# A second DMA queue for the weight tiles converted beside attention, in a float64-weight attention and gated-MLP kernel

## The chip, the cores and the metric

One Trainium2 chip, one core of it. The metric is the device time of one launch in microseconds. Five engines run programs of their own in order: TensorE (PE, with its weight loads as PEld), VectorE (DVE), ScalarE (ACT), GpSimd (POOL) and SyncE (SP). A data transfer is an instruction of the engine that begins it; the 16 DMA engines then move the bytes.

## The reference

Batch 4, 12 heads, 448 positions, head size 64, so 1792 tokens of width 768:

```python
scores = q @ k.T / sqrt(64) - log(448)
x = (sigmoid(scores) @ v) laid out as (1792, 768)
h = x @ w_in;  x = (h * cos(h)) @ w_out                   # w_in 768 x 2048
g = x @ w_gate; x = (silu(g) * (x @ w_val)) @ w_out2       # 768 x 1536, 1536 x 768
```

q, k and v are float32. The weights are float64, eight bytes an element, and the kernel must turn them into float32 itself.

## The kernel before

**Stages.** Attention comes first, in 24 steps of two heads each ("pairs", the loop in `attention`). Then layer 1 (two halves of the tokens, eight chunks of w_in and w_out each) and layer 2 (two halves, six chunks). TensorE does every float32 product as three products of a high and a low part; the layers use a seven-product scheme for 2 x 2 blocks (`seven`), and its sums of weight blocks are made by `combine` (L509) on VectorE or GpSimd.

**Conversion of weights.** `conversions` (L419) takes one tile of 128 x 768 float64 at a time from a list in order of need: it loads the raw words (768 KB, `move`, L235), scales the low words on ScalarE, takes the absolute value of the high words on VectorE or ScalarE (`absolute`, L409), does four more steps on VectorE, and stores 384 KB of float32 to a scratch tensor in HBM. There are 68 such tiles. Later `loads` brings float32 tiles back from scratch and `operands` splits them.

Some of it runs beside attention: `lend_pool` (L388) lends four pairs of buffers (`lr` raw, `lt` result) and starts four copies of `conversions` that get them as `raw`, `t` and `back`. Each copy converts tile after tile in its own buffers until it sees `stop`, which is set after pair 17; after pair 21 the buffers' memory is used for something else. Copies without `back` start after attention, with two raw buffers.

**What sets the order of instructions.** A planner (`Order`) runs while the program is written. Every task yields an engine with a planned cost, or a wait; `run` takes the task that could start first by the plan (then the lowest rank) and emits its instruction. What one engine does is therefore a fixed list. Attention's own instructions are written out by hand, and `beside` (L633, called at L778 and L781) tells the planner how long they hold each engine in a pair of planned length 5.8: SyncE for the first 2.0, VectorE for 1.75, ScalarE until 4.55 and again for 0.55 at the end. The planner fills what is left. Planned time starts at 0, the first pair at 6.0. A transfer of `move` is planned as 0.8 of SyncE, and what it brings as there 5.0 later.

**Attention's transfers.** `load` (L702) brings the queries and keys of a pair (`rqk`, two halves, four buffers) and its values (`vs`, five buffers) three pairs ahead, and `load_last` the last value rows of six pairs, all begun by SyncE except one half at the very start that ScalarE begins. `split` (L720) makes high and low parts on VectorE (L723, L724), `scores` (L734) and `weigh` (L748) are TensorE's work of a pair, and the sigmoid (L738) is ScalarE's.

Of the kernel before, what the change touches and what calls it, by code (L numbers as in the profile page):

```python
# [11 lines left out]
I32 = mybir.dt.int32  # L12
# [138 lines left out]
def block_kernel(  # L151
# [11 lines left out]
    nc = tc.nc  # L163
    P = 128
    B, NP, D, _, _, S = qk.shape
# [15 lines left out]
    def f32(ap):  # L181
        return ap.bitcast(F32)

    def flat(ap):
        return ap.rearrange("p k c -> p (k c)")
# [40 lines left out]
    def act(time, **kw):  # L226
        return {"ACT": time}, lambda _: nc.scalar.activation(**kw)  # L227

    def vec(time, out, in0, in1, op):
        return {"DVE": time}, lambda _: nc.vector.tensor_tensor(out=out, in0=in0, in1=in1, op=op)  # L230
# [4 lines left out]
    def move(out, in_):  # L235
        return {"SP": 0.8}, lambda _: nc.sync.dma_start(out=out, in_=in_)

    LANDING = 5.0
    PAIR = 5.8
    ENDS = ((17, 21),)  # L240
# [89 lines left out]
    def by(time, step):  # L330
        return (*step, time)
# [56 lines left out]
    def lend_pool():  # L388

        pool = tc.tile_pool(name="ln", bufs=1, side="right")  # L390
        ln, stop, backs = pool.__enter__(), [], []
        for a in range(4):
            raw = ln.tile([P, WT, 2], I32, tag=f"lr{a}", name=f"lr{a}")
            t = ln.tile([P, WT], F32, tag=f"lt{a}", name=f"lt{a}")
            backs.append(order.event())
            order.spawn(conversions(raw, t, backs[-1], stop), end)

        def swap():
            assert all(back.time is not None for back in backs)
            pool.__exit__(None, None, None)  # L400
            xr = ctx.enter_context(tc.tile_pool(name="xr", bufs=1, side="right"))
            x1 = xr.tile([P, 3 * size + 2 * WT + 32], F32R, tag="x1", name="x1")
            give_x(x1, ORDER[4:])
            pairs.give(x1[:, 3 * size + 16:3 * size + 16 + 2 * WT].rearrange("p (m a k c) -> p m a k c", m=2, a=2, k=KH))
            x_open.set()

        return stop, swap

    def absolute(t, words):  # L409
        def do(engine):  # L410
            if engine == "ACT":
                nc.scalar.activation(out=t, in_=words.bitcast(F32), func=AF.Abs)
            else:
                nc.vector.tensor_scalar(
                    t.bitcast(I32), words, 0, 0x7FFFFFFF, op0=ALU.logical_shift_left, op1=ALU.bitwise_and
                )
        return {"ACT": 0.9, "DVE": 0.58}, do

    def conversions(raw=None, t=None, back=None, stop=None):  # L419

        while not stop:
            w, f = next(todo, (None, 0))
            if w is None:
                break
            if not back:
                raw = yield raws
            time = uses[id(w), f]
            yield move(raw.rearrange("p n two -> p (n two)"), flat(w[f]).bitcast(I32))
            yield LANDING
            yield by(time, act(0.9, out=raw[:, :, 0], in_=raw[:, :, 0].bitcast(U32), func=AF.Copy, scale=2.0 ** -29))  # L430
            if not back:
                t = yield convs
            ti = t.bitcast(I32)
            yield by(time, absolute(t, raw[:, :, 1]))
            yield by(time, ({"DVE": 0.56}, lambda _: nc.vector.tensor_scalar(
                t, t, HI_MOST, HI_LEAST, op0=ALU.min, op1=ALU.max
            )))
            yield {"DVE": 0.56}, lambda _: nc.vector.tensor_scalar(
                ti, ti, 3, 0x3FFFFFF8, op0=ALU.logical_shift_left, op1=ALU.bitwise_and
            ), time  # L440
            yield {"DVE": 0.96}, lambda _: nc.vector.scalar_tensor_tensor(
                out=ti, in0=raw[:, :, 1], scalar=-0x40000000, in1=ti,
                op0=ALU.bitwise_and, op1=ALU.bitwise_or,
            ), time
            yield by(time, vec(0.97, ti, ti, raw[:, :, 0], ADD))
            if not back:
                raws.give(raw)
            there = scratch[id(w), f]
            there[0] = dram.tile([P, KD * P], F32, tag=f"s{names[id(w)]}{f}", name=f"s{names[id(w)]}{f}")
            yield move(there[0], t)  # L450
            order.spawn(landed(there[1], None if back else t), 0)
        if back:
            yield LANDING
            back.set()
            return

        raw = yield raws
        room = raw.rearrange("p n two -> p (n two)").bitcast(F32)
        free_t.give((yield convs))
        if not ended:  # L460
            ended.append(True)
            free_t.give(room[:, :WT])
            free_t.give(room[:, WT:])
        else:
            for a in range(3):
                tmps.give(room[:, a * N:(a + 1) * N])

    def landed(event, t=None):
        if t is not None:
            yield 3.0  # L470
            convs.give(t)
            yield LANDING - 3.0
        else:
            yield LANDING
        event.set()
# [30 lines left out]
    def operands():  # L506
# [16 lines left out]
        def lower(keys, s, t, lo, hi, size, room, free, done):  # L523
# [10 lines left out]
            if kept:  # L534
                there = dram.tile(list(s.shape), F32, tag=f"k{len(stash)}", name=f"k{len(stash)}")
                stash[at] = there, order.event()
                yield {"SP": 0.8}, (lambda _: nc.sync.dma_start(out=there, in_=f32(s))), due[keys[0]]
                yield LANDING
                stash[at][1].set()
# [17 lines left out]
        def here(keys, s, room, done):  # L557
            yield LANDING
            for i, key in enumerate(keys):
                event = made_event(key)  # L560
                made[key][1] = (s, i, room)
                event.set()
# [485 lines left out]
    with tc.manual_schedule():  # L1048
        nc.gpsimd.memset(warm, 0.0)
        for s in range(n_stages):  # L1050
            order.spawn(inputs(s), 3.5)
        order.spawn(loads(), 3)
        order.spawn(operands(), 4)
        order.spawn(banker(), 2)
        attention()
        with tc.tile_pool(name="mp", bufs=1) as mp:
            for i in range(2):
                raws.give(mp.tile([P, WT, 2], I32, tag=f"raw{i}", name=f"raw{i}"))
                order.spawn(conversions(), end)
            convs.give(mp.tile([P, WT], F32, tag="cv", name="cv"))  # L1060
            convs.give(ring[:, 2])
            make_pairs(mp, 3, "b")
            mp.tile([P, 16], F32, tag="pad", name="pad")
            for i in range(4):
                gslots.give(mp.tile([P, 2, N], F32R, tag=f"g{i}", name=f"g{i}"))
            for i in range(6):
                (tmps if i < 5 else rounds).give(mp.tile([P, N], F32, tag=f"u{i}", name=f"u{i}"))
            free_t.give(mp.tile([P, WT], F32, tag="t3", name="t3"))
            order.spawn(tensor_engine(), 0)
            order.run()  # L1070
            assert not order.open
# [51 lines left out]
```

## Time and profile before

| | us |
|---|---|
| median of 3 runs | 1088.21 |
| lowest, highest | 1086.23, 1089.68 |
| the profiled execution | 1090.07 |
| its span, first to last instruction | 1087.9 |

| engine | busy us | share |
|---|---|---|
| PE | 1067.5 | 98% |
| DVE | 846.4 | 78% |
| ACT | 664.3 | 61% |
| POOL | 126.4 | 12% |

The profile page gives busy time by engine over the span; a stretch of the span can be asked for by itself, and there the granted TensorE clock (1.00 is full speed) and the share of the DMA engines' time stand beside it. The chain of waits follows the work that ended last back to its start. A timeline lists one engine's instructions in order, with the idle time before each in square brackets and what ended it. An engine name with q (SPq) is the engine's queue of instructions that begin transfers.

### The profile page before, as it was taken

Reading aid. Unit: us, or ns where it says so; the run is one execution under the profiler, and the core shown is the slowest. Engines: PE = TensorE matmul, PEld = TensorE weight load, DVE = VectorE, ACT = ScalarE, POOL = GpSimd, SP = SyncE. Lnnn points to the kernel's source line nnn. Section 1 sums busy time; section 2 is a strip of 40 time slices with the busy share of each in tenths; the row PEclk is TensorE's granted clock in tenths of the full one; section 3 lists DMA queues with packets and bytes.
Section 4 is the critical chain, followed back from the end, with each engine's and each line's share of the span. In section 5 each row is a group of like instructions: output and inputs, shape, how many; then the busy total and the mean of one; then the engine's idle time right before and its main releaser. Section 6 shows DMA issues by size and latency. Waiting matters only on the chain.

```text
span 1087.9 us, 14759 instructions
## 1 busy us (share of the span) xinstructions
PE 1067.5 (98%) x5507; PEld 930.7 (86%) x5507; DVE 846.4 (78%) x1138; ACT 664.3 (61%) x1005; POOL 126.4 (12%) x97
## 2 busy tenths in 40 slices
PE   8999999999999899999997999999999999999998
PEld 4554569999989799999997999999999999999997
DVE  4969759989999989989899988887559644655644
ACT  6787768877777777777776665554345444433330
POOL 0100003001111101100023111111111110110100
PEclk9999999999999999999998999999999999999999
DMA  9999524545654146454513566565122322112002
GB/s 260 300 268 238 155 87 146 201 148 174 218 203 146 58 170 206 161 175 145 189 59 132 176 213 205 189 194 171 43 73 76 124 78 73 59 45 73 30 1 102
DMA packets 64455, 156.68 MB, mean 144 GB/s; under 512 B 10112, under 2 KB 36736, under 8 KB 64384
## 3 DMA queue, kind: packets, MB, share of 16 engines
q1 hardware_dynamic: 64240, 155.51, 45.3%
q8 instruction: 43, 0.70, 0.3%
q10 hardware_dynamic: 144, 0.23, 0.1%
q14 instruction: 28, 0.23, 0.1%
HBM read 123.47 MB, written 32.24 MB: 143 GB/s over the span
## 4 chain that ended last, share of the span: by engine, by line
PE 86%; DVE 9%; DMA 2%; issue 1%; ACT 1%; SPq 1%; DVEq 0%; ACTq 0%
PE banks L1000 42%; PE banks L902 33%; PE banks L748 6%; PE banks L734 5%; DVE x L230 2%; DVE r L230 2%; DMA rqk<-in_qk 2%; DVE u L230 1%; DVE g L230 1%; DVE wa L230 1%; DVE wb L230 0%; DVE u L816 0%; DVE s L230 0%; DVE x L660 0%; SPq L707 0%
## 5 line engine op out<-in xcount | busy, mean ns | idle before, releaser
L902 PE MATMUL banks<-g,wb 128*128 128x448 f32 x1044 | 224.5, 363 | 1.1 <-ACT g L227 0.5
L1000 PE MATMUL banks<-x,wb 128*128 128x448 f32 x1044 | 225.0, 363 | 0.1
L902 PEld LDWEIGHTS banks<-g,wb 128*128 128x128 f32 x1044 | 195.6, 188 | 15.8 <-ACT g L227 1.4
L1000 PEld LDWEIGHTS banks<-x,wb 128*128 128x128 f32 x1044 | 195.9, 188 | 14.6 <-ACT banks L227 0.5
L902 PE MATMUL banks<-g,wa 128*128 128x448 f32 x720 | 159.9, 369 | 9.9 <-ACT g L227 8.4
L1000 PE MATMUL banks<-x,wa 128*128 128x448 f32 x738 | 160.6, 363 | 0.0
L902 PEld LDWEIGHTS banks<-g,wa 128*128 128x128 f32 x720 | 137.6, 192 | 21.4 <-ACT g L227 9.1
L1000 PEld LDWEIGHTS banks<-x,wa 128*128 128x128 f32 x738 | 138.3, 188 | 11.1 <-issue 0.7
L227 ACT ACTIVATE u<-u 128x448 f32<-128x448 f32 x179 | 99.4, 570 | 38.9 <-DVE u L230 26.3
L230 DVE TENSOR_TENSOR u<-u,banks 128x448 f32<-128x448 f32 x119 | 73.4, 617 | 58.2 <-PE banks L1000 54.8
L230 DVE TENSOR_TENSOR r<-banks,r 128x896 f32<-128x896 f32 (+1 forms) x69 | 74.2, 1076 | 53.4 <-PE banks L902 52.9
L738 ACT ACTIVATE a<-banks 128x896 f32<-128x896 f32 x96 | 82.7, 922 | 20.6 <-PE banks L734 12.1
L230 DVE TENSOR_TENSOR wb<-t,wb 128x768 fp32r<-128x768 f32 x73 | 69.5, 957 | 14.8 <-ACT wb L227 14.4
L227 ACT ACTIVATE g<-u 128x448 fp32r<-128x448 f32 x97 | 55.1, 572 | 39.8 <-DVE u L230 24.7
L1000 PE MATMUL banks<-x,s 128*128 128x448 f32 x360 | 79.3, 364 | 0.0
L734 PEld LDWEIGHTS banks<-qk 64*128 64x128 f32 x576 | 50.3, 185 | 31.2 <-ACT a L738 9.4
L512 POOL TENSOR_TENSOR sum<-t 128x384 f32<-128x384 f32 x20 | 36.6, 1832 | 339.7 <-DMA t<-swi 147.3
L227 ACT ACTIVATE wb<-t 128x768 fp32r<-128x768 f32 x73 | 60.8, 836 | 24.5 <-PE banks L1000 17.7
L734 PE MATMUL banks<-qk 64*128 64x448 f32 x576 | 69.4, 382 | 4.7 <-ACT a L738 2.6
L227 ACT ACTIVATE r<-banks 128x896 f32<-128x896 f32 x52 | 47.8, 919 | 40.6 <-PE banks L902 40.6
L1000 PEld LDWEIGHTS banks<-x,s 128*128 128x128 f32 x360 | 67.5, 187 | 5.3
L227 ACT ACTIVATE banks<-banks 128x448 f32<-128x448 f32 x80 | 42.3, 529 | 47.6 <-PE banks L1000 46.6
(103 smaller groups left out, 1474.5 us busy)
## 6 DMA issues: line engine op xcount, KB each, us to landing
raw<-in_w_out SPq DMA_DIRECT2D x23, 768.0 KB, 5.0
t<-swi SPq DMA_DIRECT2D x32, 384.0 KB, 3.2
t<-swo SPq DMA_DIRECT2D x64, 192.0 KB, 2.7
rqk<-in_qk SPq DMA_DIRECT2D x47, 224.0 KB, 8.1
raw<-in_w_gate SPq DMA_DIRECT2D x12, 768.0 KB, 4.7
raw<-in_w_val SPq DMA_DIRECT2D x12, 768.0 KB, 4.6
t<-swg SPq DMA_DIRECT2D x18, 384.0 KB, 3.0
t<-swd SPq DMA_DIRECT2D x34, 192.0 KB, 2.8
```

Source lines behind the costliest of these rows:

```text
L227: return {"ACT": time}, lambda _: nc.scalar.activation(**kw)
L230: return {"DVE": time}, lambda _: nc.vector.tensor_tensor(out=out, in0=in0, in1=in1, op=op)
L512: on.tensor_tensor(out=out, in0=a, in1=b, op=op)
L734: nc.tensor.matmul(sc[:, j], lhsT=both[half, m, 1, starts[c]:starts[c] + P], rhs=both[half, p, 0], start=n == 0, stop=n == 2,)
L738: nc.scalar.activation(out=a, in_=sc, func=AF.Sigmoid, bias=-math.log(S), scale=1.0 / math.sqrt(D))
L748: nc.tensor.matmul(o[half], lhsT=value, rhs=a[:, j], start=c == 0, stop=c == NCH)
L902: nc.tensor.matmul(banks[:, first + e - d, :N], lhsT=w[:, m, e % KH, :], rhs=g[:, p], start=(i, m, p) == (0, 0, 0) and is_fresh and not pr ...
L1000: nc.tensor.matmul(bank, lhsT=w[:, m, k, :], rhs=x[:, k, p, :], start=(k, m, p) == (0, 0, 0) and i in (1, 5), stop=(k, m) == (KH - 1, 1), ...
```

## The change

The raw load and the store of a tile converted beside attention (a copy of `conversions` that has `back`) are begun by GpSimd, with a planned cost of 1.1 of GpSimd; those of the tiles converted after attention stay with SyncE.

```diff
+    def move_beside(out, in_):
+        return {"POOL": 1.1}, lambda _: nc.gpsimd.dma_start(out=out, in_=in_)
+
...
             time = uses[id(w), f]
-            yield move(raw.rearrange("p n two -> p (n two)"), flat(w[f]).bitcast(I32))
+            convey = move_beside if back else move
+            yield convey(raw.rearrange("p n two -> p (n two)"), flat(w[f]).bitcast(I32))
             yield LANDING
...
-            yield move(there[0], t)
+            yield convey(there[0], t)
             order.spawn(landed(there[1], None if back else t), 0)
```

## Rows read from the trace of the kernel before

**Rows 1.** The page, part 4: shares of the chain that ended last.

```profile
PE 86%; DVE 9%; DMA 2%; issue 1%; ACT 1%; SPq 1%; DVEq 0%; ACTq 0%
```

**Rows 2.** Busy time by stretch; the stretch's length first, then engines, clock, DMA share.

```profile
0.00:155.00 155.00, 149.15 (x972) 77.97 (x973) 114.42 (x136) 113.00 (x142) 5.51 (x9) 0.99 0.82 217
...
320.00:400.00 80.00, 75.80 (x367) 69.66 (x366) 75.14 (x96) 60.88 (x96) 11.89 (x9) 0.98 0.36 117
...
585.00:620.00 35.00, 29.33 (x135) 26.38 (x134) 30.68 (x42) 23.46 (x37) 13.95 (x6) 0.90 0.55 192
```

**Rows 3.** Timeline of PE in attention: start, length, line, count, idle time before.

```profile
28.77 0.47 PE L734 MATMUL banks<-qk 64*128 64x448 f32 x2
29.78 2.63 PE L734 MATMUL banks<-qk 64*128 64x448 f32 x22 [0.54 <-DVE qk L724]
...
94.60 2.83 PE L734 MATMUL banks<-qk 64*128 64x448 f32 x24
97.36 2.48 PE L748 MATMUL banks<-a,vs 128*64 128x448 f32 x12
...
104.76 1.28 PE L734 MATMUL banks<-qk 64*128 64x448 f32 x6 [2.15 <-ACT a L738]
105.97 3.68 PE L748 MATMUL banks<-a,vs 128*64 128x448 f32 x12
```

**Rows 4.** Who waited for whom, 0 to 150 us: total, times, longest.

```profile
DVE qk L723 <- DMA rqk<-in_qk: 19.4, 8, 5.4
...
ACT x L658 <- DVE r L230: 2.8, 1, 2.8
```

**Rows 5.** Timeline of DVE in attention.

```profile
8.37 0.63 DVE L723 CAST qk<-rqk 128x896 fp32r<-128x896 f32 x1 [0.92 <-DMA rqk<-in_qk]
...
75.20 0.63 DVE L723 CAST qk<-rqk 128x896 fp32r<-128x896 f32 x1 [3.69 <-DMA rqk<-in_qk]
...
85.31 1.55 DVE L660 CAST x<-r 128x1344 fp32r<-128x1344 f32 x1
```

**Rows 6.** Timeline of SP's queue in attention.

```profile
7.36 1.48 SPq L707 DMA_DIRECT2D rqk<-in_qk  x2
...
9.95 2.67 SPq L236 DMA_DIRECT2D lr<-in_w_in  x4
...
18.60 3.98 SPq L707 DMA_DIRECT2D rqk<-in_qk  x2
...
26.86 0.34 SPq L236 DMA_DIRECT2D swi<-lt  x1
```

**Rows 7.** Instructions on the lent raw buffers: count, ns, first and last start.

```profile
L227 ACT ACTIVATE lr<-lr x13: 922/934/953, 16.7 to 115.0; 128x768 int32<-128x768 uint32 x13
```

**Rows 8.** VectorE's instructions on the lent result buffers: least, median, most ns.

```profile
L435 DVE TENSOR_SCALAR lt<-lt x13: 551/554/1361, 18.8 to 122.8; 128x768 f32<-128x768 f32 x13
...
L441 DVE SCALAR_TENSOR_TENSOR lt<-lr,lt x13: 950/957/959, 20.0 to 124.0; 128x768 int32<-128x768 int32 x13
```

**Rows 9.** Early stretches as in rows 2; DMA share and GB/s are last.

```profile
2.80:3.40 0.60, 0.60 (x4) 0.18 (x2) 0.00 (x0) 0.12 (x1) 0.00 (x0) 1.00 1.05 370
3.40:4.40 1.00, 1.00 (x4) 0.41 (x3) 0.00 (x0) 0.00 (x0) 0.00 (x0) 1.00 1.07 231
14.00:16.00 2.00, 2.00 (x14) 0.72 (x10) 0.00 (x0) 0.92 (x1) 0.00 (x0) 1.00 1.03 410
```

**Rows 10.** DMA queues from 2.8 to 3.4 us: packets, MB, share (q10 ScalarE's, q1 SyncE's).

```profile
q10 hardware_dynamic: 100, 0.15, 68.1%
q1 hardware_dynamic: 38, 0.07, 37.1%
```

**Rows 11.** Timeline of POOL.

```profile
49.17 1.44 POOL L512 TENSOR_TENSOR sum<-t 128x384 f32<-128x384 f32 x1 [48.33 <-DMA t<-swi]
50.69 1.74 POOL L512 TENSOR_TENSOR t<-t 128x384 f32<-128x384 f32 x1
```

**Rows 12.** Timeline of DVE beside it.

```profile
49.78 1.78 DVE L724 TENSOR_TENSOR qk<-rqk,qk 128x896 fp32r<-128x896 f32 x1
```

## The prediction, made before the changed kernel had run

> **What bounds the kernel now.** I read the page's chain first. 86% of it is TensorE [rows 1], so a change counts only where TensorE stands still. The busy times by stretch show where that is: the 155 us of attention hold 149.15 us of PE, the stretch around 360 us lacks 4.2 us and the one around 600 us 5.67 us [rows 2]; the rest of the span up to the last stage has next to nothing. The change touches transfers of attention only, so I took the timeline of PE there. After the first pairs it has two marks [rows 3]. At 28.77 a score group that takes 2.83 us elsewhere lasts until 32.41, 0.81 us lost, because a split waited for its queries and keys. At 104.76 PE had been idle for 2.15 us, and the twelve products behind it take 3.68 us where 2.48 is usual, 1.20 us more: TensorE had stood still, and for a moment it ran slower. Together 4.16 us.
>
> Both marks lead to SyncE's queue. VectorE's splits waited 19.4 us in eight places for `rqk` [rows 4], among them 3.69 us at 75.20 [rows 5]. From there to the stop at 104 VectorE has no gap longer than an instruction's start, its work on the layers' input begins only at 85.31 [rows 5], and ScalarE's part of that waits 2.8 us for it [rows 4], with a sigmoid behind it that TensorE needs. The splits waited since SyncE begins everything in one order: four raw tiles stand ahead of later pairs' loads, a pair of load instructions takes 3.98 us to get rid of at 18.60, and the first store holds the queue until 26.86 [rows 6]. The DMA engines are full at this time (a share of 1.03 to 1.07 [rows 9]).
>
> **The change, part by part.**
>
> *Removed from SyncE:* 13 raw loads and 13 stores [rows 7], with their waits. Then attention's loads wait for free buffers alone, and are begun up to three pairs ahead. I expect the waits of 19.4 us to go mostly. At 28.77 that repays 0.81. At 104 it repays the 3.69 us that VectorE lost at 75.20, and 1.9 us of that reach the input work: pairs last (94.60 - 29.58) / 11 = 5.91 us [rows 3], so pair 13 began at 82.8, and the result that the work needs was there some 0.6 later, not at 85.31. Of 2.15 us some 0.25 stays idle, and the slow stretch of 1.20 goes. Sum -3.9; bounds 0 (the waits move from queries to raw tiles, as the DMA engines are no less full) and -4.16. What is late next there is ScalarE, which the plan gives one conversion instruction a pair.
>
> *Moved, the first four raw tiles.* They depend on nothing. On SyncE they come behind four pairs' loads, at 9.95 [rows 6]; as the first work of GpSimd after a small memset they begin at about 1 us, and 4 x 0.79 MB lie beside the very loads that the first pairs wait for. One queue alone moves attention's rows at 231 GB/s and the big rows of raw tiles at 410; the only moment with two queues moved 370 [rows 9]. So a second queue adds throughput, but it also takes turns. If SyncE's queue keeps 231 GB/s, the cost is 0. If the raw tiles go first, it is 3.15 MB / 410 GB/s = 7.7 us. In between: if a row of each goes in turn, a row of 1792 bytes lasts 77 ns at 370/16 GB/s an engine and one of 6144 bytes 240 ns at 410/16, so SyncE gets 1792/317 ns x 16 = 90 GB/s. Pair 1's loads behind the first (192 + 448 KB, 0.66 MB) then last 7.3 us instead of 2.8; its split, which started at 8.37 [rows 5], comes 4.5 us later, with no slack, as its scores follow pair 0's at once. The raw tiles are through by about 13 us, so pair 2 pays no more. In the one row of two queues they were not served alike, 100 packets to 38 [rows 10], so neither end is excluded. I take 4.0, near the middle, because GpSimd's first transfer also needs its own start. A stop of that length is followed by a slow stretch like that at 104.76: +1.2, bounds 0 and 2.4 (two stops).
>
> *The trains of conversion.* Planned starts follow from the code: SyncE was reserved to 2.0 of each pair, so the four loads were planned inside pair 0 and ScalarE's first step fell in pair 1 (16.7 [rows 7]). GpSimd is unreserved, the loads are planned at 0.15, 1.25, 2.35 and 3.45, and the first step fits pair 0. Everything then runs a pair earlier, until VectorE turns to the input work. By the stop after pair 17 nine stores had been planned, so 4 + 9 tiles were taken; a tenth now fits before the input work, and I expect 14. The extra one is 3.6 us of VectorE (two steps of 0.957 us and three of 0.554 [rows 8]) in attention, where VectorE has 155 - 114.4 = 40.6 us idle [rows 2]: nothing. Later, 54 tiles in place of 55 are converted over some 586 us; the two places where TensorE lacks time (80 and 35 us [rows 2]) are 20% of that, 0.2 x 3.6 = 0.7. I take -0.7; but another tile count makes the planner order all the rest anew, so the bounds are -4.2 (the first place cleared) and +5.7 (a second one like 600).
>
> *Added to GpSimd:* 28 transfers. No row shows one begun there. The nearest are its own combines, 1.44 and 1.74 us [rows 11], and SyncE's store, 0.34 us [rows 6]; at 0.3 to 1.7 us each they fill 9 to 49 us of a GpSimd that is busy 5.51 us of 155 [rows 2]. I take 1.1 each, the plan's own figure. A store on GpSimd waits for the last VectorE step of its tile; behind it stand the same buffers' next load, harmless with four pairs of buffers, and a combine for the first weight blocks, which nothing in attention needs. A combine waiting as at 49.17 (its tile landed late [rows 11]) holds raw loads back by a microsecond or two. Cost 0; without the cover of four buffers ScalarE and TensorE would wait that long, about 2 us.
>
> Sum: -3.9 + 4.0 + 1.2 - 0.7 + 0 = +0.6 against the profiled 1090.07, so 1090.7. That execution lies 1.86 above the median of 1088.21, hence 1088.8.
>
> *A rule against it.* Beside GpSimd's second combine VectorE's split step took 1.78 us [rows 12], and one conversion step 1361 ns where 554 is the median [rows 8]: the two engines hold each other up by 0.7 to 0.8 us. The Trainium skill, SBUF — State Buffer, Who interferes with whom, goes further: a transfer begun by GpSimd is itself starved while VectorE runs certain one-input instructions in its two-port mode, and the advice is to begin it on another engine. No row here shows that for a transfer. As a mechanism of this kernel it is the third rival.
>
> **The rivals.**
>
> 1. *Free start, faster.* SyncE's queue keeps its 231 GB/s beside GpSimd's, or GpSimd begins late. For it: two queues moved 370 GB/s [rows 9]. Against it: 100 to 38 [rows 10]. Then no 4.0 and no 1.2: -4.2 - 0.7 = -4.9, 1083.3.
> 2. *Raw tiles first, slower.* Place: pairs 0 to 2. Price 7.7, and two slow stretches, 2.4; since TensorE is then later than everything else, the 4.16 goes entirely: 7.7 + 2.4 - 4.2 - 0.7 = +5.2, 1093.4. It decides from a start cost of some 7 us, where it passes what the later stops give back by 0.3%. Against it: the first loads are under way before GpSimd's.
> 3. *Ports, slower.* Each transfer costs VectorE 0.7 us. From 75.2 to 104 is five pairs with 28/20 transfers each, 7 x 0.7 = 4.9 us where VectorE has no gap, so the stop at 104 is not repaid but grows: +0.6 + 3.9, about 1092.7.
> 4. *Nothing changes hands.* The waits for queries turn into waits for raw tiles, TensorE's stops stay, the start is free: 1088.2. It counts with "same".
> 5. *Another order.* The later stages come out anew by up to -4 or +5 around any of these.
>
> **Chances.** Forecast and 4: 0.37. Rival 1, and forecast with a lucky order: 0.35. Rivals 2, 3 and an unlucky order: 0.13, 0.08, 0.07. A difference of 0.3%, 3.3 us, is about what can be told from no change: faster 0.35, same 0.37, slower 0.28. The likeliest case alone runs from 1085.5 to 1091.5; with both sides 1080 to 1097.
>
> **What would show it.** A second queue of 28 transfers, 16 MB, from about 1 us; SyncE's queue without stores; splits' waits for `rqk` after 28 us near 0; PE idle around 10 us and none at 28 and 104; 14 tiles in `lr`, the first ScalarE step near 10 us. Wrong would be: pair 1's split before 9 us (start free), VectorE's conversion steps above their medians throughout (ports), 13 tiles, or a changed loss around 360 and 600 us larger than attention's.

## The result: 1.1% slower, and the profile after

| | us |
|---|---|
| before, median of 6 runs | 1087.55 |
| changed kernel, median of 6 runs (1098.21 to 1100.47) | 1099.89 |
| ratio, with its 95% interval | 1.011 (1.0096 to 1.0124) |
| the profiled execution of the changed kernel, and its span | 1099.17, 1097.4 |

The prediction was 1088.8 in a range of 1080 to 1097: wrong, by 11 us.

The changed kernel's page, part 3, shows that the change does what it says: a queue of its own (q0) carries 16.52 MB, 28 transfers of 14 tiles.

```profile
q1 hardware_dynamic: 60208, 139.00, 39.7%
q0 software_dynamic: 3136, 16.52, 4.3%
```

Its busy time by stretch has the columns of [rows 2]. The place near 360 us lacks 4.65 us where it lacked 4.2, the place near 600 us lacks 12.16 where it lacked 5.67, and attention's clock has fallen to 0.97.

```profile
0.00:155.00 155.00, 146.59 (x957) 79.54 (x959) 117.85 (x142) 114.02 (x141) 21.45 (x36) 0.97 0.77 224
...
320.00:400.00 80.00, 75.35 (x359) 69.14 (x358) 73.81 (x96) 61.51 (x96) 16.95 (x9) 0.96 0.31 99
...
585.00:620.00 35.00, 22.84 (x104) 20.41 (x103) 29.99 (x41) 21.63 (x33) 6.48 (x4) 0.80 0.44 150
```

The timeline of PE, to be read against [rows 3]: the stops at 28 and 104 us are gone, and one of 4.98 us at the start and one of 11.57 us near 600 stand in their place. The first line after the second "..." is pair 2's scores, the next the first products of layer 1, so attention's end; L1004 is what was L1000, L738 what was L734.

```profile
7.46 4.05 PE L738 MATMUL banks<-qk 64*128 64x448 f32 x22 [0.65 <-DVE qk L728]
16.48 0.74 PE L738 MATMUL banks<-qk 64*128 64x448 f32 x2 [4.98 <-DVE qk L727]
17.52 4.30 PE L738 MATMUL banks<-qk 64*128 64x448 f32 x22 [0.29 <-DVE qk L728]
...
24.91 2.84 PE L738 MATMUL banks<-qk 64*128 64x448 f32 x24
...
157.95 2.09 PE L1004 MATMUL banks<-x,wa 128*128 128x448 f32 x9
...
587.34 1.98 PE L1004 MATMUL banks<-x,s 128*128 128x448 f32 x9
600.89 0.74 PE L906 MATMUL banks<-g,wa 128*128 128x448 f32 x1 [11.57 <-ACT g L227]
602.22 3.84 PE L906 MATMUL banks<-g,wa 128*128 128x448 f32 x11 [0.59 <-DVE g L230]
```

The same marks in the kernel before:

```profile
16.40 2.09 PE L734 MATMUL banks<-qk 64*128 64x448 f32 x18
...
154.71 2.09 PE L1000 MATMUL banks<-x,wa 128*128 128x448 f32 x9
...
584.27 1.98 PE L1000 MATMUL banks<-x,s 128*128 128x448 f32 x9
591.89 5.04 PE L902 MATMUL banks<-g,wa 128*128 128x448 f32 x12 [5.64 <-ACT g L227]
```

Mark against mark the changed kernel is 8.5 us late at pair 2, 3.24 at the end of attention, 3.07 ahead of the stop near 600 us, 9.0 behind it, and 9.5 at the end of the span. So two places carry it: the start of attention, of which a part is given back, and the stop near 600 us, which no transfer of the change comes near. The medians lie 12.3 apart, these two executions 9.1: the one of before was 2.5 us above its median in the table, the one of the changed kernel 0.7 below. From 25 to 155 us TensorE is now busy for all of the 130 us (127.31 before), and VectorE's splits wait 1.8 us for `rqk` from 25 to 150 us (13.7 before).

What the start is can be read from three views of the changed kernel. GpSimd begins four raw tiles at 1.31 us and is done with it by 3.6 (where [rows 6] had SyncE begin them at 9.95):

```profile
1.31 2.27 POOL L239 DMA_DIRECT2D lr<-in_w_in  x4 [0.45 <-issue]
24.21 0.83 POOL L239 DMA_DIRECT2D swi<-lt  x1 [20.63 <-DVE lt L230]
```

Pair 1's split starts at 15.71 where [rows 5] had it at 8.37:

```profile
15.71 0.63 DVE L727 CAST qk<-rqk 128x896 fp32r<-128x896 f32 x1 [8.31 <-DMA rqk<-in_qk]
```

And the DMA queues from 8 to 10 us (packets, MB, share, as in [rows 10]) move almost the same number of packets each, but 0.54 MB against 0.16:

```profile
q0 software_dynamic: 104, 0.54, 76.8%
q1 hardware_dynamic: 107, 0.16, 26.8%
```

### The profile page after: what moved, and what is told of

The parts are those of the page before. It is cut to its first block, busy times and chain, and to the rows that moved or that the text cites. A ratio compares the mean times of both kernels' runs of the same rounds, so it can differ in the third digit from the quotient of the medians.

```text
span 1097.4 us, 14796 instructions
## 1 busy us (share of the span) xinstructions
PE 1068.0 (97%) x5507; PEld 934.1 (85%) x5507; DVE 850.5 (78%) x1132; ACT 663.4 (60%) x1002; POOL 156.2 (14%) x134
## 3 DMA queue, kind: packets, MB, share of 16 engines
q0 software_dynamic: 3136, 16.52, 4.3%
## 4 chain that ended last, share of the span: by engine, by line
PE 92%; DVE 5%; DMA 1%; issue 1%; ACT 0%; SPq 0%; DVEq 0%
PE banks L1004 44%; PE banks L906 36%; PE banks L752 7%; PE banks L738 6%; DVE x L230 1%; DMA rqk<-in_qk 1%; DVE r L230 1%; DVE u L230 1%; DVE g L230 0%; DVE u L820 0%; ACT x L662 0%; DVE wb L230 0%; DVE s L230 0%; DVE wa L230 0%; SPq L711 0%
## 5 line engine op out<-in xcount | busy, mean ns | idle before, releaser
L1004 PE MATMUL banks<-x,wb 128*128 128x448 f32 x1044 | 225.0, 363 | 0.1
L1004 PEld LDWEIGHTS banks<-x,wb 128*128 128x128 f32 x1044 | 195.7, 188 | 14.6 <-ACT banks L227 0.5
L1004 PE MATMUL banks<-x,wa 128*128 128x448 f32 x738 | 160.6, 363 | 0.0
L1004 PEld LDWEIGHTS banks<-x,wa 128*128 128x128 f32 x738 | 138.3, 188 | 11.1 <-issue 0.7
L738 PEld LDWEIGHTS banks<-qk 64*128 64x128 f32 x576 | 53.4, 194 | 32.8 <-ACT lr L227 8.5
L1004 PE MATMUL banks<-x,s 128*128 128x448 f32 x360 | 79.3, 364 | 0.0
L738 PE MATMUL banks<-qk 64*128 64x448 f32 x576 | 71.7, 394 | 7.2 <-DVE qk L727 6.3
L1004 PEld LDWEIGHTS banks<-x,s 128*128 128x128 f32 x360 | 67.5, 187 | 5.3
L230 DVE TENSOR_TENSOR g<-u,g 128x448 fp32r<-128x448 f32 x98 | 63.7, 658 | 8.5 <-ACT g L227 8.4
```

Source lines behind the costliest of these rows:

```text
L738: nc.tensor.matmul(sc[:, j], lhsT=both[half, m, 1, starts[c]:starts[c] + P], rhs=both[half, p, 0], start=n == 0, stop=n == 2,)
L1004: nc.tensor.matmul(bank, lhsT=w[:, m, k, :], rhs=x[:, k, p, :], start=(k, m, p) == (0, 0, 0) and i in (1, 5), stop=(k, m) == (KH - 1, 1), ...
```

## The experiments

Each was timed in five rounds beside the kernel before, the last one excepted. "Order" is the order of instructions that the planner writes.

**The order without the queue, and the queue without the order.** Three kernels. `e1_order` keeps the changed kernel's plan and gives the transfers back to SyncE:

```diff
     def move_beside(out, in_):
-        return {"POOL": 1.1}, lambda _: nc.gpsimd.dma_start(out=out, in_=in_)
+        return {"POOL": 1.1}, lambda _: nc.sync.dma_start(out=out, in_=in_)
```

> The changed kernel's order on TensorE, VectorE and ScalarE, and its 14 tiles, but the lent tiles' transfers are begun by SyncE again (planned as before-change GpSimd work at 1.1). Theory O (two costs: the early raw loads hold up pair 2's queries, about 3 us; and the tile count of 14 gives the later stages another order, whose stop near 600 us grows from 5.6 to 11.6 us): the stop near 600 us is 9 to 12 us here too, and from the end of attention to the end of the span it is 6 us longer than before. At the start ScalarE's first conversion step now stands ahead of pair 1's sigmoids while its tile lands at some 16 us, so attention itself may lose 2 to 5 us for another reason; the time 1094 to 1100. Rival Q (the later loss comes from GpSimd's queue or from ports, not from the order): the stop near 600 us is 5 to 6 us as before, the time 1087 to 1092.

`e2_queue` keeps the plan of before and gives the transfers to GpSimd:

```diff
     def move_beside(out, in_):
-        return {"POOL": 1.1}, lambda _: nc.gpsimd.dma_start(out=out, in_=in_)
+        return {"SP": 0.8}, lambda _: nc.gpsimd.dma_start(out=out, in_=in_)
```

> The order and the 13 tiles of the kernel before (planned as SyncE's work at 0.8), but the lent tiles' transfers are begun by GpSimd. Theory O: a stop of 4 to 6 us for pair 2's queries at about 12 us as in the changed kernel, the stops of before at 28 and 104 us gone, attention 2 to 4 us longer than before, everything later as before: 1089 to 1092. Rival Q: later stages lose 6 us although their order is that of before: 1096 to 1100. Rival P (ports): VectorE's conversion steps in attention above their medians of 554 and 957 ns.

`e3_thirteen` is the changed kernel with a limit:

```diff
         while not stop:
+            if back:
+                taken.append(True)
+                if len(taken) > 13:
+                    break
             w, f = next(todo, (None, 0))
```

> The changed kernel with one edit: no more than 13 tiles are taken beside attention. Theory O: the later stages have the order of before again, so the stop near 600 us is 5 to 6 us, the start pays as in the changed kernel: 1088 to 1092, 8 to 11 us under the changed kernel. Rival Q: 1097 to 1100 as the changed kernel.

| | median us | ratio to before, 95% |
|---|---|---|
| e1_order | 1099.1 | 1.0090 (1.0066 to 1.0113) |
| e2_queue | 1094.3 | 1.0049 (1.0033 to 1.0066) |
| e3_thirteen | 1094.37 | 1.0049 (1.0033 to 1.0066) |

The stop near 600 us follows the tile count and not the queue. It is 11.56 us in `e1_order`, whose lent transfers are SyncE's:

```profile
599.84 0.74 PE L906 MATMUL banks<-g,wa 128*128 128x448 f32 x1 [11.56 <-ACT g L227]
```

and 5.64, that of before, in `e3_thirteen`, whose transfers are GpSimd's:

```profile
596.72 5.25 PE L912 MATMUL banks<-g,wa 128*128 128x448 f32 x12 [5.64 <-ACT g L227]
```

One tile fewer takes 1099.89 - 1094.37 = 5.5 us off the changed kernel; by the two ratios, each to the kernel before of its own rounds, it is 6.6. `e2_queue` and `e3_thirteen` agree with each other: that is the price of the queue alone, 6.0 us by the medians and 5.3 by the ratios, above what both expectations gave (1089 to 1092 and 1088 to 1092). `e1_order` is as slow as the changed kernel through a coincidence that its expectation allowed for: with ScalarE's first step planned in pair 0 and its tile landing late, a sigmoid queued behind it holds TensorE for 5.75 us until 18.21 us (ScalarE itself waits 4.91 us for that tile). The rival that the later loss needs GpSimd's queue is refuted. So is the ports' rival; it is taken up below.

**14 tiles without any of it.** `e6_before14` is the kernel before with one number changed.

```diff
-    ENDS = ((17, 21),)
+    ENDS = ((18, 21),)
```

> The kernel before with one number changed, so that the lent buffers stop taking tiles a pair later (18 in place of 17): 14 tiles, every transfer begun by SyncE, the start untouched. The order of the layers on TensorE is then that of the changed kernel. Theory O: the stop near 600 us is 11 to 12 us, attention's length as before, 1092 to 1096. Rival Q (that stop needs GpSimd's queue or the late start): 5 to 6 us there, 1086 to 1090.

Measured: 1094.03, ratio 1.0064 (1.0043 to 1.0085). The timeline of PE:

```profile
338.82 0.47 PE L902 MATMUL banks<-g,wa 128*128 128x448 f32 x1 [2.82 <-ACT g L227]
...
594.87 0.74 PE L902 MATMUL banks<-g,wa 128*128 128x448 f32 x1 [11.56 <-ACT g L227]
```

The stops at 340 and near 595 us are those of the changed kernel to a hundredth or two (2.83 and 11.57). A fourteenth tile by itself costs 6 us; no transfer changed hands.

What fills the longer stop can be read on VectorE, which has no gap in it in either kernel. In the changed kernel (the stop is from 589.32 to 600.89) three splits of weight blocks and four steps of conversions lie inside it, 5.45 us together:

```profile
589.25 0.95 DVE L230 CUSTOM_DVE_ANT_0 t<-raw,t 128x1536 uint16<-128x1536 uint16 x1
590.12 0.55 DVE L439 TENSOR_SCALAR cv<-cv 128x768 f32<-128x768 f32 x1
...
592.59 0.95 DVE L230 TENSOR_TENSOR x<-t,x 128x768 fp32r<-128x768 f32 x1
593.46 0.95 DVE L230 TENSOR_TENSOR wb<-t,wb 128x768 fp32r<-128x768 f32 x1
...
594.86 0.95 DVE L230 TENSOR_TENSOR wa<-t,wa 128x768 fp32r<-128x768 f32 x1
...
597.33 0.55 DVE L442 TENSOR_SCALAR cv<-cv 128x768 int32<-128x768 int32 x1
...
598.34 0.55 DVE L417 TENSOR_SCALAR t<-raw 128x768 int32<-128x768 int32 x1
```

In the kernel before (the stop is from 586.25 to 591.89) three such splits come ahead of it, and one conversion step lies at its end:

```profile
583.31 0.94 DVE L230 TENSOR_TENSOR x<-t,x 128x768 fp32r<-128x768 f32 x1
584.17 0.95 DVE L230 TENSOR_TENSOR wb<-t,wb 128x768 fp32r<-128x768 f32 x1
...
585.58 0.94 DVE L230 TENSOR_TENSOR wa<-t,wa 128x768 fp32r<-128x768 f32 x1
...
591.13 0.94 DVE L230 CUSTOM_DVE_ANT_0 t<-raw,t 128x1536 uint16<-128x1536 uint16 x1
```

The stop grew by 5.93 us. `e6_before14` has the changed kernel's seven instructions inside its stop too.

**Is a tile more what hurts, or any other order?** `e9_twelve` is the kernel before with the limit above set to 12, `e10_before15` the kernel before with another rank for conversions:

```diff
-                uses.setdefault((id(w), 2 * c + i), due[key] - 25.0)
+                uses.setdefault((id(w), 2 * c + i), due[key] - 15.0)
```

> The kernel before, but no more than 12 tiles are taken beside attention; all transfers by SyncE. If a tile more beside attention is what hurts the layers, 12 are better than 13: 1083 to 1087. If it is only that the planner makes another order, for which the kernel's numbers were not chosen, 12 may be as bad as 14: the stops of TensorE after attention sum to more than the 10 us of before, 1091 to 1098.

> The kernel before with one number of the plan changed: the rank of a tile's conversion is its use less 15 in place of less 25. No transfer changes hands. If the layers' loss is a matter of the order that the planner falls into, this gives other stops after attention too; in its order TensorE should wait in three places (near 307, 360 and 587 us) in place of five. 1084 to 1089, faster if the place near 587 us stays at 5 to 6 us.

`e9_twelve` took 1099.8, ratio 1.0089 (1.0062 to 1.0116), above its range at the top. TensorE stops in six places after attention; the longest:

```profile
232.93 0.47 PE L908 MATMUL banks<-g,wa 128*128 128x448 f32 x1 [2.10 <-ACT g L227]
...
375.54 0.74 PE L908 MATMUL banks<-g,wa 128*128 128x448 f32 x1 [5.42 <-ACT g L227]
...
602.38 5.25 PE L908 MATMUL banks<-g,wa 128*128 128x448 f32 x12 [5.64 <-ACT g L227]
```

`e10_before15` took 1087.21, ratio 0.9987 (0.9972 to 1.0003): no difference that counts. Its two stops:

```profile
362.76 0.74 PE L902 MATMUL banks<-g,wa 128*128 128x448 f32 x1 [4.46 <-ACT g L227]
...
589.06 5.13 PE L902 MATMUL banks<-g,wa 128*128 128x448 f32 x12 [5.64 <-ACT g L227]
```

So neither more nor fewer tiles is good in itself: by the medians 12 cost 11.8 us and 14 cost 6.0 against 13 (9.7 and 7.0 by the ratios). The planner writes another order for each, and of the three orders tried beside this kernel's two were slower and one no different.

**What the queue costs at the start.** `e8_small` is `e2_queue` with the first four raw loads cut into quarters of their columns.

```diff
+    def move_parts(out, in_):
+        def do(_):
+            n = in_.shape[1] // 4
+            for part in range(4):
+                cols = slice(part * n, (part + 1) * n)
+                nc.gpsimd.dma_start(out=out[:, cols], in_=in_[:, cols])
+        return {"SP": 0.8}, do
...
-            yield convey(raw.rearrange("p n two -> p (n two)"), flat(w[f]).bitcast(I32))
+            if back:
+                taken.append(True)
+            yield (move_parts if back and len(taken) < 5 else convey)(raw.rearrange("p n two -> p (n two)"), flat(w[f]).bitcast(I32))
```

> As the run with the order of before and GpSimd's queue, but each of the first four raw loads is begun as four transfers of a quarter of the columns, rows of 1536 bytes in place of 6144. If the two queues take turns row by row, SyncE's rows now get half the bytes: pair 1's split starts at 9 to 12 us (15.7 there), pair 2's scores at 17 to 20 us (25.7 there), the time 1086 to 1090. If GpSimd's queue is served first whatever the rows: 14 us or later, 1092 to 1096.

Measured: 1092.0, ratio 1.0039 (1.0024 to 1.0053), 2.3 us under `e2_queue` by the medians and 1.1 by the ratios, whose intervals overlap, so the gain in time is not shown. In the profiles pair 1's split moves from 15.71 to 12.07, pair 2's scores from 25.67 to 22.55, attention's end from 158.71 to 155.63: the direction of turns row by row, but less than expected. The queues of `e8_small` from 8 to 10 us:

```profile
q0 software_dynamic: 97, 0.32, 65.0%
q1 hardware_dynamic: 115, 0.19, 38.2%
```

GpSimd's packets now hold 0.32 MB / 97 = 3.3 KB in place of the changed kernel's 0.54 / 104 = 5.2 KB, not 1.5: the rows were a quarter as long but the packets did not shrink as much. The packet counts stay near one to one, and SyncE's queue goes only from 80 to 95 GB/s. That the two queues alternate packet by packet fits both runs from 6 us on; why the packets hold two rows is open. Nor does this run change the rows alone: GpSimd begins the 16 parts one after another until 14.68 us, from the ninth on after waiting for earlier ones to land, where `e2_queue` had begun all four tiles by 3.56. And from 4 to 6 us SyncE's queue moved 0.22 MB where it had moved 0.04 in `e2_queue`, so part of the gain lies ahead of the even turns.

**What of SyncE's queue made the queries late?** `e7_stores` gives GpSimd only the 13 stores, in the order of before. `e4_queue_start` gives it the stores and all raw loads but the first four.

```diff
# e7_stores
-            yield move(there[0], t)
+            yield (move_beside if back else move)(there[0], t)
# e4_queue_start
-            yield convey(raw.rearrange("p n two -> p (n two)"), flat(w[f]).bitcast(I32))
+            if back:
+                taken.append(True)
+            yield (move_first if back and len(taken) < 5 else convey)(raw.rearrange("p n two -> p (n two)"), flat(w[f]).bitcast(I32))
```

Here `move_beside` costs SyncE 0.8 in the plan and is begun by GpSimd; `move_first` is `move`.

> The kernel before with its order, in which GpSimd begins the 13 stores alone; the raw loads stay with SyncE. If SyncE's waits for stores are what made the queries late, the stops at 28 and 104 us shrink and attention is 1 to 4 us shorter: 1084 to 1087.5. If the raw tiles ahead of them in the ring are: no change, 1087 to 1089.5.

> As the run with the order of before, but the first four raw loads stay with SyncE, behind four pairs' loads; the other 9 raw loads and all 13 stores are begun by GpSimd. Theory O: no stop at 12 us, and the stops at 28 and 104 us are smaller or gone: attention 1 to 4 us shorter than before, 1083 to 1087. If the later stops were not SyncE's doing: 1087 to 1089. Rival P: 1090 and more.

`e7_stores`: 1088.69, ratio 1.0003 (0.9991 to 1.0015). Its stop of attention is still there:

```profile
105.17 0.87 PE L737 MATMUL banks<-qk 64*128 64x448 f32 x6 [1.93 <-ACT a L741]
```

`e4_queue_start`: 1089.76, ratio 1.0006 (0.9992 to 1.0019), short of the expected 1083 to 1087. The stop at 104 us is gone, and others have come at 54 and 61 us. Ahead of the first VectorE waits 4.60 us for queries, while GpSimd's queue moves 0.35 to 0.57 MB in each 2 us from 42 to 54 us and SyncE's 0.15 to 0.30. Ahead of the second it waits for nothing, but two of its steps take 1.55 and 1.75 us where 0.96 and 0.95 are usual, beside GpSimd's combines of 56.70 to 59.60 us:

```profile
54.02 0.47 PE L745 MATMUL banks<-qk 64*128 64x448 f32 x2 [1.41 <-DVE qk L734]
55.05 2.63 PE L745 MATMUL banks<-qk 64*128 64x448 f32 x22 [0.56 <-DVE qk L735]
61.10 0.47 PE L745 MATMUL banks<-qk 64*128 64x448 f32 x2 [0.26 <-DVE qk L734]
...
153.62 2.09 PE L1011 MATMUL banks<-x,wa 128*128 128x448 f32 x9
```

So the stores were not it, and of the raw loads the first four are the whole price of the queue: with them left behind, the second queue costs and brings nothing that can be told. `e11_start15` puts this start and the rank of 15 together:

> The same rank of less 15, and the first four raw loads begun by SyncE, the other raw loads and the stores by GpSimd, with the order of the plan in which both cost SyncE 0.8. If the gains add: attention about 1 us shorter than before and the layers as in the run with the rank alone, 1083 to 1088. If the turns of the two queues take back what the freed queue gives: as the run with the rank alone.

It took 1092.38, ratio 1.0034 (1.0019 to 1.0048): slower, and neither of its two parts by itself had a gain clear of noise to add. TensorE waits 3.38 us for a sigmoid in the same region:

```profile
59.60 1.22 PE L745 MATMUL banks<-qk 64*128 64x448 f32 x6 [3.38 <-ACT a L749]
```

This is another chain than in `e4_queue_start`: ScalarE had stood for 5.51 us until 57.01, ahead of that sigmoid, for a sum that GpSimd's combine makes, and the combine at 55.99 had waited for its float32 tile to land. In `e10_before15` the same step of ScalarE starts at 51.91 without a wait. So a late combine can hold attention, which the prediction had put at nothing.

**The kernel before again.**

> The kernel before once more, for a second profile. Its timed runs spread over some 4 us and its profiled execution is 2 us above their median. If attention's stops depend on how the transfers of one ring happen to land, the end of attention differs from 154.7 us by 1 to 3 us and the stops after it are the same 10 us.

One execution, 1090.65. Attention ends at 155.17 and the stops after it are those of before:

```profile
155.17 2.09 PE L1000 MATMUL banks<-x,wa 128*128 128x448 f32 x9
...
592.39 5.17 PE L902 MATMUL banks<-g,wa 128*128 128x448 f32 x12 [5.64 <-ACT g L227]
```

This second profile is again above the median. With all transfers on SyncE and the start of before, attention ended at 154.71 and 155.17 here and at 155.80 in `e9_twelve`, but at 152.23 in `e6_before14` and 151.52 in `e10_before15`; with GpSimd's early raw loads it ended at 157.95, 158.38 and 158.71. Of the 2.5 us between the kernel before and `e6_before14`, 2.0 arise at the stop near 104 us: it is 2.15 us and the granted clock from 100 to 120 us is 0.91 in the one, 1.80 us and 1.00 in the other, and the two pairs that it falls in take 15.72 and 13.77 us. If most runs of the kernel before end attention near 152, a price of 6 us in the medians fits beside 3.2 to 4.0 in the profiles. It is an inference: no profile shows a run of the kernel before at its median.

## Why the prediction was wrong

**Another order: the step that failed.** The walk through the plan was right: 14 tiles, with ScalarE's first step at 12.4 us, behind pair 0's sigmoids, where it was 16.7 [rows 7]:

```profile
L227 ACT ACTIVATE lr<-lr x14: 867/940/954, 12.4 to 124.1; 128x768 int32<-128x768 uint32 x14
```

Its price was not. I set -0.7, the extra tile's 3.6 us of VectorE times the 20% of time in which TensorE waits, and gave an unlucky order a chance of 0.07. The runs say +5.5 to 6.6 (`e3_thirteen` against the changed kernel) and +6.0 to 7.0 (`e6_before14` against before), by medians and by ratios. My own upper bound had been +5.7, "a second one like 600"; what came was that stop doubled. The error was to price a new order by the work that it removes. With VectorE busy for 30.68 of the 35 us around 600 us [rows 2], what TensorE waits for there depends on which of VectorE's instructions stands before which, and three weight splits and four conversion steps now lie inside the stop. Two neighbouring counts differ by 6 and 12 us from this one. Two of three other orders tried lost and none won; a new order should have had a larger share of the chances than 0.07 on the slower side. One of my signs of being wrong came true: the loss around 360 and 600 us changed by 0.45 + 6.49 us, more than the 3.24 by which attention ended later.

**The start: right place, size too small.** I took 4.0 + 1.2 between 0 and 7.7 + 2.4; measured at pair 2 it is 8.5, about 6.0 of it the stop itself and 2.5 the score group behind it (16.48 to 21.75 us, 5.27 where [rows 3] has 2.76). Pair 1's split comes 7.3 us late where I worked out 4.5. The rate was nearly right (0.16 MB in 2 us are 80 GB/s, I had 90), but SyncE's queue fared worse before that. The queues from 4 to 6 us:

```profile
q0 software_dynamic: 88, 0.54, 93.0%
q1 hardware_dynamic: 29, 0.03, 8.8%
```

There are two slow stretches, at a granted clock of 0.50 from 8 to 10 and from 18 to 20 us: 22 products take 4.05 and 4.30 us where 2.63 is usual for as many [rows 3]. Only the second costs time. The first lies ahead of the 4.98 us stop; in `e2_queue` those 22 products take 2.56 us, the stop is 6.53, and pair 1's scores begin at 16.48 just the same. I had given "its own start" of GpSimd as a ground for the middle; the transfers began at 1.31 us, 0.45 behind its memset. Rival 2's 7.7 + 2.4 lies 1.6 above the 8.5, my 5.2 lies 3.3 below it.

**What the later stops give back: more than bounded, cause open.** I took -3.9, with -4.16 as the bound; of 8.5 us late at pair 2, 3.24 are left at the end of attention, so 5.3 came back in these two profiles. 3.90 of it are at 104 us (I had 3.35), 0.82 at 28, and 0.53 at a stop of 0.41 us at 18.90 that I had left out. I put the return down to a SyncE queue without raw loads and stores. `e7_stores`, without the stores alone, keeps the stop at 104. In `e4_queue_start`, without the stores and nine raw loads, that stop is gone, but TensorE is by then 2.8 us later than before; in the changed kernel it is 7.1 us later. No run has the freed queue with TensorE on time, so whether the stops go because the queries come earlier or because TensorE comes later, as rival 2 had it, is not shown.

**GpSimd's transfers** took 0.53 to 0.92 us each for a load, and 0.54 to 0.89 for a store, where I took 1.1; they are on no path. VectorE's conversion steps in attention show nothing of the ports' rival: all medians are within 2 ns of those before, and the longest of the step that took 1361 ns in the kernel before [rows 8] is 561:

```profile
L439 DVE TENSOR_SCALAR lt<-lt x14: 551/554/561, 20.7 to 127.1; 128x768 f32<-128x768 f32 x14
```

The Trainium skill's rule that such a transfer starves beside VectorE (SBUF — State Buffer, Who interferes with whom) is shown by no run here: at most the 0.3 to 0.4 us between the shortest and the longest could be that, and they delay nothing. On the start, the Trainium skill states that each DMA engine takes the queues in turn, a packet of one and then of the next (DMA: Bandwidth & Descriptors, Queues, rings and completion order). 104 to 107 packets from 8 to 10 us, one queue's with a third of the other's bytes, fit that rule if the profile's packet is the page's, which no run here shows; 88 to 29 from 4 to 6 us do not fit it.

The sum: +0.6 forecast; measured +12.3, of which the order is 5.5 to 6.6 and the queue 5.3 to 6.1 (`e2_queue` and `e3_thirteen`, by ratios and by medians).

## What to carry to other kernels

Work that depends on nothing can start as soon as it has a queue of its own (here at 1.31 us in place of 9.95): before moving a transfer, ask what it will then run ahead of, and count bytes per turn, since here a queue with rows three times as large took three times the bandwidth from 8 to 10 us. Where a planner writes the order, a change of a cost or a queue can change a count far away; price the new order as a draw with the spread that neighbouring settings show, not by the work that it saves, and test it with the order and the queue each held fixed.

## What the hardware showed that was not expected

- Two queues of 1.8 KB and 6 KB rows shared packets about one to one from 6 to 14 us (83 to 110 of SyncE's beside 87 to 121 of GpSimd's in each 2 us), bytes one to three or four; but in the 2 us before that the queue of GpSimd had 88 packets to 29.
- Cutting the rows of a GpSimd transfer from 6144 to 1536 bytes left packets of two rows: the first four raw tiles went in 576 packets for 512 rows in `e2_queue` and in 1024 packets for 2048 rows in `e8_small`.
- With GpSimd's large rows beside SyncE's small ones the DMA engines moved 406 GB/s from 6 to 8 us and 317 to 351 from 8 to 14, where SyncE's queue alone had moved 223 to 236 from 6 to 14.
